# A routed expert layer behind attention on one core: weight casts, result turns and products in another order at each slot boundary

## The chip, the cores and the metric

The kernel runs on one core of a Trainium2 chip. The metric is the device time of one execution in microseconds (us). Before the change it was 924.96 us, the median of three runs from 918.28 to 929.62.

## What is computed

Attention with a causal mask and a decay bias on 8 x 8 heads of 576 x 64, then a two-level routed layer on the 4608 rows of 512 that come out of it: each row goes to the best of 4 groups and then to the best of 4 experts in it, and that expert (512 x 1024, relu, 1024 x 512) works on the row alone.

```python
scores = np.where(causal, -1e9, scale * q @ k.T + np.minimum(bias, 0.0))
x = (softmax(scores) @ v)            # rows of 512
g_idx = np.argmax(x @ w_group, axis=1)
for g in range(4):
    e_idx = np.argmax(xg @ w_expert[g], axis=1)
    for e in range(4):
        h = np.maximum(xg[mask_e] @ w1[g, e], 0.0)
        ye = h @ w2[g, e]
        out[tok_idx] = combined[:, None] * ye      # softmax weights of group and expert
```

## The kernel before

The first half of the span is attention and the routing that goes with it; the change leaves it alone. After it come 16 **slots**, one for each expert, the experts sorted by how many rows they got: slot k takes at most `CAPS[k]` rows, 368 in slot 1, falling to 256 in slots 14 and 15. The loop over slots 1 to 15 stands at L1463. All products are done to near fp32 accuracy from two halves: a tensor a is split into ah, its rounding to fp32r, and al = a - ah, and a product of a and b is ah x bh + al x bh + ah x bl, three matmuls.

For slot k the loop issues two halves:

- The **first half** (`h_items`, L1084): 8 items of 12 matmuls (L1107), item f giving 128 hidden columns in PSUM (ph). Behind each item ScalarE makes hh = relu(ph) rounded (L1102) and VectorE hl = relu(ph) - hh (L1103).
- The **second half** (`y_items`, L1147): 4 items of 24 matmuls (L1168), one for each 128 columns of y; ScalarE copies each out of PSUM into yT (L1165, L1179). Within the first item the products with hh come first (16), then the eight with hl. Where the cap is a multiple of 128 (slots 14 and 15) `y_rows` (L1120) takes another way, row blocks at once.

Beside these products three jobs run in pieces that the loop puts between the items:

- **W: the weights of the next slot.** Four tiles of 128 x 2048 (two of w1, two of w2) are loaded by the SP queue, each cut in four pieces, W[0] to W[15]. A piece is cast by ScalarE to wh (L997). Its low part wl is either subtracted by GpSimd (L1000), or ScalarE casts it once more into a PSUM tile pw (L1005) and VectorE subtracts that (L1007). For the last two tiles pieces 0 and 2 go to VectorE and pieces 1 and 3 to GpSimd. A tile's buffer is loaded anew three tiles later.
- **X: the rows of the next slot.** They have been gathered by a GpSimd DMA into xg (L953). In slots 2 to 14 sixteen 32 x 32 block transposes of VectorE turn them into xt (L1074; eight items of two), then two split items make xh (ScalarE, L1078) and xl = xt - xh (VectorE, L1079), half the columns each. Slots 1 and 15 use TensorE transposes (px, L1057) instead.
- **Z: the result of the slot before.** Sixteen VectorE transposes turn yT back into rows yr (L1221; eight items of two), then ScalarE scales them in two or three blocks (`leave`, L1224), and a GpSimd DMA scatters each (L958).

TensorE, VectorE and ScalarE run in the order in which the code is written (a manual schedule, L1462); a waiting instruction holds all that stand behind it on its engine. GpSimd's order and the SP queue's are the scheduler's. In the first half Z[i] and W[i] follow item i (L1468); in the second half four X items and two W pieces stand ahead of each of the first items, so X's two split items and W[12], W[13] stand ahead of item 2 and W[14], W[15] ahead of item 3 (L1478).

Of the kernel before, what the change touches and what calls it, by code (L numbers as in the profile page):

```python
# [8 lines left out]
F32 = mybir.dt.float32  # L9
# [4 lines left out]
ALU = mybir.AluOpType  # L14
# [6 lines left out]
P = 128  # L21
# [3 lines left out]
E = 16  # L25
# [67 lines left out]
def after(tc, *instructions):  # L93

    stack = ExitStack()
    for i in instructions:
        if i is not None:
            stack.enter_context(tc.issue_after(i.ins))
    return stack
# [824 lines left out]
def moe(tc, w1, w2, xs, st, out):  # L924
    nc = tc.nc
    V = nc.vector
    ident, mc = st.ident, st.cst
    with ExitStack() as ctx:
# [40 lines left out]
        class Expert:  # L969


            def __init__(self, u, e):
                self.u, self.e = u, e
                self.h, self.l, self.casts = [], [], []

            def load(self, hi=(None,) * 4, lo=(None,) * 4, eng=V):

                pieces = []

                with after(tc, *(loads[-1:] if 0 < self.u < E else ())):  # L980
                    e = nc.values_load(self.e, engines=[ENG.SP], min_val=0, max_val=E - 1)
                for i, w in enumerate((w1, w1, w2, w2)):

                    turn = 4 * self.u + i
                    q, n = (x1, 2) if turn % 3 < 2 else (x2, 1)
                    raw = q.tile([P, 4, 512], F32, name=f"raw{self.u}_{i}", tag="raw", bufs=n)
                    q, n = (wp, 4) if turn % 6 < 4 else (wq, 2)
                    h = q.tile([P, 4, 512], F32R, name=f"wh{self.u}_{i}", tag="wh", bufs=n)
                    l = q.tile([P, 4, 512], F32R, name=f"wl{self.u}_{i}", tag="wl", bufs=n)
                    self.h.append(h)  # L990
                    self.l.append(l)

                    def piece(j, i=i, w=w, raw=raw, h=h, l=l):
                        if j == 0:
                            loads.append(nc.sync.dma_start(raw, w[bass.ds(e, 1), i % 2].rearrange("o p a c -> p (o a) c")))
                        with after(tc, hi[i], lo[i]):
                            self.casts.append(nc.scalar.copy(h[:, j], raw[:, j]))  # L997

                            if (j in ((1, 2, 3) if i < 2 else (1, 3)) if eng is V else (i, j) not in lent):
                                self.low = lows[self.u, i, j] = nc.gpsimd.tensor_tensor(out=l[:, j], in0=raw[:, j],  # L1000
                                                                   in1=h[:, j].bitcast(F32), op=ALU.subtract)
                                return

                            ps = turn_in(f"pw{self.u}_{i}_{j}", F32R)
                            nc.scalar.copy(ps, raw[:, j])  # L1005
                            with after(tc, None if eng is V else st.valued if i == 2 else st.cut):
                                lows[self.u, i, j] = V.tensor_tensor(out=l[:, j], in0=raw[:, j], in1=ps.bitcast(F32),  # L1007
                                                                     op=ALU.subtract)

                    pieces += [lambda j=j, piece=piece: piece(j) for j in range(4)]  # L1010
                return pieces
# [10 lines left out]
        def acc(name):  # L1022

            turns[0] += 1
            return pm[turns[0] // 2 % 2].tile([P, 512], F32, name=name, tag="pm")
# [11 lines left out]
        class Slot:  # L1037
# [12 lines left out]
            def x_items(self):  # L1050
                u, cap = self.u, self.cap
                self.xh, self.xl = xhl(u, 0 if u == 0 else u + 1)

                def item(c):
                    ps = acc(f"px{u}_{c}") if u == 0 else turn_in(f"px{u}_{c}")
                    for t, r in enumerate(self.rows):
                        nc.tensor.transpose(ps[:, t * P:t * P + r], self.xg[:r, t, c * P:(c + 1) * P], ident[:r, :r])  # L1057
                    self.split = (nc.scalar.copy(self.xh[:, c, :cap], ps[:, :cap]),
                                  V.tensor_tensor(out=self.xl[:, c, :cap], in0=ps[:, :cap],
                                                  in1=self.xh[:, c, :cap].bitcast(F32), op=ALU.subtract))  # L1060

                if u < 2 or u == E - 1:
                    return [lambda c=c: item(c) for c in range(4)]

                xt = turned(u)
                nb = -(-cap // 32)

                def turn(j, i0):

                    n = len(range(j, nb, 4))  # L1070
                    for i in (i0, i0 + 1):
                        src = self.xg[32 * j:32 * j + 32].rearrange("p t (c i n) -> p t c i n", c=4, n=32)
                        dst = xt[32 * i:32 * i + 32].rearrange("p c (t j n) -> p t c j n", j=4, n=32)
                        V.transpose(dst[:, 0:n, :, j], src[:, 0:n, :, i])  # L1074

                def split(a):
                    xh, xl, x = (t[:, a:a + 2, :cap] for t in (self.xh, self.xl, xt))
                    nc.scalar.copy(xh, x)  # L1078
                    V.tensor_tensor(out=xl, in0=x, in1=xh.bitcast(F32), op=ALU.subtract)  # L1079

                return ([lambda j=j, i=i: turn(j, i) for j in range(4) for i in (0, 2)] +
                        [lambda a=a: split(a) for a in (0, 2)])

            def h_items(self):  # L1084
                u, cap = self.u, self.cap
                self.hh = hp.tile([P, 8, 384], F32R, name=f"hh{u}", tag="hh")
                self.hl = hp.tile([P, 8, 384], F32R, name=f"hl{u}", tag="hl")

                pss = {}

                def first(f):

                    pss[f] = acc(f"ph{u}_{f}")
                    for c in range(4):
                        for x in (self.xh, self.xl):
                            product(f, self.w.h, x, c)

                def last(f):
                    for c in range(4):
                        product(f, self.w.l, self.xh, c)  # L1100
                    ps, hh = pss.pop(f), self.hh[:, f, :cap]
                    self.rounded = self.rounds[f] = nc.scalar.activation(hh, ps[:, :cap], AF.Relu)  # L1102
                    self.rests[f] = V.scalar_tensor_tensor(out=self.hl[:, f, :cap], in0=ps[:, :cap], scalar=0.0,  # L1103
                                           in1=hh.bitcast(F32), op0=ALU.max, op1=ALU.subtract)

                def product(f, w, x, c):
                    self.product = nc.tensor.matmul(pss[f][:, :cap], w[f // 4][:, c, (f % 4) * P:(f % 4 + 1) * P], x[:, c, :cap],  # L1107
                                     start=(c == 0 and w is self.w.h and x is self.xh), stop=(c == 3 and w is self.w.l))

                def item(f):  # L1110
                    first(f)
                    last(f)

                if u == 0:

                    return [lambda f=f, part=part: part(f) for h in (0, 4) for part in (first, last)
                            for f in range(h, h + 4)]
                return [lambda f=f: item(f) for f in range(8)]
# [169 lines left out]
        def run(items):  # L1288
            for f in items:
                f()  # L1290
# [171 lines left out]
        with tc.manual_schedule(engines={ENG.PE, ENG.DVE, ENG.Activation}):  # L1462
            for k in range(1, E):  # L1463
                W = wts[k + 1].load() if k + 1 < E else []
                rest = beyond() if k + 1 == E else iter(())
                for i, f in enumerate(slots[k].h_items()):
                    f()
                    run(Z[i:i + 1] + W[i:i + 1])  # L1468
                    if k == 1 and i == 2:
                        by_slot(cws, cwl, 1, E)  # L1470
                    for _ in range(4):
                        next(rest, None)
                    if i == 4 and k + 2 < E:
                        slots[k + 2].gather()
                X = slots[k + 1].x_items() if k + 1 < E else []
                for i, f in enumerate(slots[k].y_items()):
                    n = 1 if k + 2 == E else 4
                    run((Z[8:] if i == 0 else []) + X[n * i:n * i + n] + W[8 + 2 * i:10 + 2 * i])  # L1478
                    f()
                Z = slots[k].z_items()  # L1480
            run(Z)
# [166 lines left out]
```

## Time and profile before

| | |
|---|---|
| Median of three runs | 924.96 us |
| The profiled execution's time | 921.04 us |
| Its span, first to last instruction | 919.3 us |
| TensorE matmul busy / weight load busy | 855.2 us (93%) / 780.2 us (85%) |
| VectorE busy | 736.9 us (80%) |
| ScalarE busy | 610.2 us (66%) |
| GpSimd busy | 605.7 us (66%) |
| Mean granted clock of TensorE | 0.986 of full speed |

How to read it: the shares are means over two very different halves. Slot 1 starts its products at 500.1 us; from slot 2 on (530.26 us) a slot is 24 to 30 us long, and what counts there is read slot by slot. Engines: PE is TensorE's matmul, PEld its weight load, DVE is VectorE, ACT is ScalarE, POOL is GpSimd. Successive matmuls start 0.12 to 0.17 us apart, while each is shown as 0.28 to 0.33 us long and its weight load as 0.19: the shown ends of matmuls reach into a wait behind them, those of weight loads hardly do.

### The profile page before, as it was taken

What the parts mean: (1) busy time and instruction counts of PE and PEld (TensorE: products, weight loads), DVE (VectorE), ACT (ScalarE), POOL (GpSimd) and SP (SyncE); (2) the same over time, 40 slices, a digit from 0 to 9 for tenths busy, and PEclk for the clock granted to TensorE, in tenths of its full rate; (3) what the DMA queues carried; (4) which work ended last, traced back from release to release, by engine and by line L of the source; (5) the groups of instructions that cost most, each with busy time, mean ns of one, the idle gap of its engine ahead of it and who ended that gap; (6) DMA issues with size and microseconds to landing.
All of it is one profiled execution on the core that took longest, in us unless ns stands there. A gap on an engine that the chain in (4) does not pass through costs nothing. (4 is left out here: it accounts for less than half of the span.)

```text
span 919.3 us, 17750 instructions
## 1 busy us (share of the span) xinstructions
PE 855.2 (93%) x5584; PEld 780.2 (85%) x5584; DVE 736.9 (80%) x1981; ACT 610.2 (66%) x1389; POOL 605.7 (66%) x748
## 2 busy tenths in 40 slices
PE   4899999999999999998798999999999999999995
PEld 2778788788888888886687999999999999999984
DVE  7666697787979798777578888899888899888871
ACT  5667777677777777775646566666767666767750
POOL 9666567666776758546665856766676776767650
PEclk9999999999999999999899999999999999999998
DMA  7899888888888888622544645545555545655510
GB/s 204 236 238 227 215 230 227 206 210 200 220 223 217 221 223 214 160 74 100 189 150 168 221 176 205 193 169 190 215 185 191 195 183 205 229 197 192 181 70 24
DMA packets 81877, 174.06 MB, mean 189 GB/s; under 512 B 9676, under 2 KB 45132, under 8 KB 73584
## 3 DMA queue, kind: packets, MB, share of 16 engines
q1 hardware_dynamic: 71664, 152.93, 57.8%
q0 software_dynamic: 7488, 18.89, 5.8%
q10 hardware_dynamic: 2624, 1.03, 0.5%
q8 instruction: 46, 0.75, 0.4%
q14 instruction: 55, 0.45, 0.2%
HBM read 108.97 MB, written 19.69 MB: 140 GB/s over the span
## 5 line engine op out<-in xcount | busy, mean ns | idle before, releaser
L1000 POOL TENSOR_TENSOR wl<-raw,wh 128x512 fp32r<-128x512 f32 x163 | 210.3, 1305 | 76.2 <-ACT wh L997 58.5
L227 DVE CUSTOM_DVE_ANT_0 mx<-pm,mask 128x192 bf16<-128x192 f32 (+4 forms) x320 | 127.3, 418 | 36.0 <-PE pm L219 33.3
L997 ACT CAST wh<-raw 128x512 fp32r<-128x512 f32 x256 | 155.3, 616 | 1.4 <-issue 1.4
L1107 PE MATMUL ph<-xl,wh 128*128 128x256 f32 (+13 forms) x512 | 145.3, 303 | 3.0 <-DVE xl L1079 3.0
L1107 PE MATMUL ph<-xh,wh 128*128 128x256 f32 (+13 forms) x512 | 144.8, 302 | 2.0 <-ACT xh L1078 1.7
L219 PE MATMUL pm<-WA 66*128 66x288 f32 (+4 forms) x384 | 124.8, 356 | 21.5 <-DVE mc L227 11.5
L275 PE MATMUL ps<-WA 68*128 68x320 f32 (+4 forms) x384 | 135.3, 356 | 4.8 <-DMA WA<-tl 4.6
L315 PE MATMUL po<-pt,VT 128*128 128x256 f32 (+3 forms) x512 | 120.9, 355 | 6.8 <-issue 4.2
L1168 PE MATMUL py<-hl,wh 128*128 128x256 f32 (+13 forms) x448 | 113.6, 302 | 1.7 <-DVE hl L1103 1.7
L1168 PE MATMUL py<-hh,wh 128*128 128x256 f32 (+13 forms) x448 | 112.9, 302 | 0.0
L277 PE MATMUL ps<-WB 128*128 128x320 f32 (+4 forms) x384 | 109.8, 299 | 0.0
L315 PE MATMUL po<-pu,VT 128*128 128x320 f32 (+1 forms) x384 | 107.5, 388 | 1.1 <-POOL pu L294 1.1
L1221 DVE STREAM_TRANSPOSE yr<-yT 32x384 f32<-32x384 f32 (+1 forms) x208 | 104.5, 502 | 4.2
L315 PEld LDWEIGHTS po<-pt,VT 128*128 128x128 f32 x512 | 88.4, 193 | 21.0 <-issue 5.0
L1074 DVE STREAM_TRANSPOSE xt<-xg 32x256 f32<-32x256 f32 (+1 forms) x208 | 102.5, 493 | 3.1
L1107 PEld LDWEIGHTS ph<-xl,wh 128*128 128x128 f32 x512 | 96.9, 189 | 5.9 <-DVE xl L1079 5.0
L1107 PEld LDWEIGHTS ph<-xh,wh 128*128 128x128 f32 x512 | 97.1, 190 | 3.8 <-ACT xh L1078 2.9
L219 PEld LDWEIGHTS pm<-WA 66*128 66x128 f32 (+1 forms) x384 | 69.1, 192 | 31.8 <-DVE mc L227 15.5
L294 POOL TENSOR_SCALAR_AFFINE_SELECT pt<-pt 128x128 f32<-128x128 f32 (+2 forms) x192 | 65.8, 354 | 43.7 <-ACT pt L285 40.5
L1102 ACT ACTIVATE hh<-ph 128x256 fp32r<-128x256 f32 (+13 forms) x128 | 53.6, 420 | 60.3 <-PE ph L1107 59.5
L161 POOL TENSOR_TENSOR WB<-r,hl 64x576 fp32r<-64x576 f32 x62 | 87.3, 1408 | 5.9 <-ACT hl L157 2.1
L1107 PE MATMUL ph<-xh,wl 128*128 128x256 f32 (+13 forms) x512 | 90.2, 299 | 0.0
(246 smaller groups left out, 2000.8 us busy)
## 6 DMA issues: line engine op xcount, KB each, us to landing
raw<-in_w_dram SPq DMA_DIRECT2D x64, 1024.0 KB
r<-in_qk_dram SPq DMA_DIRECT2D x32, 576.0 KB
WA<-hl SPq DMA_DIRECT2D x60, 288.0 KB
WB<-hl SPq DMA_DIRECT2D x60, 288.0 KB
VT<-in_v_dram SPq DMA_DIRECT2D x32, 384.0 KB
WB<-hl SPq DMA_DIRECT2D x64, 144.0 KB
xs<-xr SPq DMA_DIRECT2D x15, 512.0 KB
WA<-cumd SPq DMA_DIRECT2D x56, 4.5 KB
```

What stands on the lines that cost most here:

```text
L161: (nc.vector if p < 1 else nc.gpsimd).tensor_tensor(out=hl[:, 2] if part else WB[p % NBB][0:64, KA, h], in0=r[hr, part], in1=hl[hr, part]. ...
L219: nc.tensor.matmul(ps[:rows, :cw], WA[i][0:66, QA, h, QO + q0:QO + q0 + rows], WA[i][0:66, KA, h, QO + c0:QO + c0 + cw], start=True, stop= ...
L227: nc.vector.tensor_tensor_reduce(out=tmp[:rows, :cw], in0=ps[:rows, :cw], in1=mk[:rows], scale=1.0, scalar=-3.0e38 if c0 == 0 else mo, op0 ...
L275: nc.tensor.matmul(ps[:rows, o:o + w], WA[i][0:68, KA, h, QO + k0:QO + k0 + rows], WA[i][0:68, QA, h, QO + q0:QO + q0 + w], start=True, st ...
L277: nc.tensor.matmul(ps[:rows, o:o + w], WB[p % NBB][:, KA, h, k0:k0 + rows], WB[p % NBB][:, QA, h, q0:q0 + w], start=False, stop=True)
L315: nc.tensor.matmul(po[0][:, qa - base:qb - base], VT[p % NVT].rearrange("p t a d -> p (t a d)")[:, (3 * t + 1 + h) * 64:][:, 0:P], x[:, c: ...
L997: self.casts.append(nc.scalar.copy(h[:, j], raw[:, j]))
L1000: self.low = lows[self.u, i, j] = nc.gpsimd.tensor_tensor(out=l[:, j], in0=raw[:, j], in1=h[:, j].bitcast(F32), op=ALU.subtract)
L1074: V.transpose(dst[:, 0:n, :, j], src[:, 0:n, :, i])
L1107: self.product = nc.tensor.matmul(pss[f][:, :cap], w[f // 4][:, c, (f % 4) * P:(f % 4 + 1) * P], x[:, c, :cap], start=(c == 0 and w is sel ...
L1168: self.product = nc.tensor.matmul(pss[c][:, :cap], w[2 + f // 4][:, f % 4, c * P:(c + 1) * P], x[:, f, :cap], start=(f == 0 and w is self. ...
L1221: V.transpose(dst[:, 0:n, :, i], src[:, 0:n, :, j])
```

## The change

Five things move; no instruction is added or taken away, apart from the order.

- The last weight tile's four pieces W[12] to W[15] are all cast ahead of item 2 of the second half, and the split items of X move from item 2 to item 3, behind those casts. The low parts of these four pieces are held in a list (`held`) and issued right behind the split.
- GpSimd's first subtract on that tile is made to wait for VectorE's second split instruction (`hold`).
- The result turns of the slot before start two items earlier: Z[0] and Z[1] ahead of item 0, Z[2] to Z[7] behind items 0 to 5.
- In slots 2 to 14 the first item of the first half takes the products with xh first (with wh and wl), then the four with xl.
- In slot 14, X's transposes on TensorE stand ahead of the scaling of slot 13's rows.

```diff
@@ class Expert, load @@
+                            def pooled():
                                 self.low = lows[self.u, i, j] = nc.gpsimd.tensor_tensor(out=l[:, j], in0=raw[:, j],
                                                                    in1=h[:, j].bitcast(F32), op=ALU.subtract)
+                            if (j in ((1, 2, 3) if i < 2 else (1, 3)) if eng is V else (i, j) not in lent):
+                                if self.held is None:
+                                    pooled()
+                                else:
+                                    self.held.append(pooled)
                                 return
...
+                            def low():
+                                with after(tc, None if eng is V else st.valued if i == 2 else st.cut):
+                                    lows[self.u, i, j] = V.tensor_tensor(out=l[:, j], in0=raw[:, j], in1=ps.bitcast(F32),
+                                                                         op=ALU.subtract)
+                            if self.held is None:
+                                low()
+                            else:
+                                self.held.append(low)
@@ class Slot, h_items @@
                 def item(f):
+                    if f == 0 and 1 < u < E - 1:
+                        pss[f] = acc(f"ph{u}_{f}")
+                        for a in (0, 2):
+                            for w in (self.w.h, self.w.l):
+                                for c in (a, a + 1):
+                                    product(f, w, self.xh, c, False)
+                        for c in range(4):
+                            product(f, self.w.h, self.xl, c, c == 3)
+                        relu(f)
+                        return
                     first(f)
                     last(f)
@@ the loop over slots @@
                 for i, f in enumerate(slots[k].h_items()):
+                    if i == 0:
+                        run(Z[:2])
                     f()
-                    run(Z[i:i + 1] + W[i:i + 1])
+                    run(Z[2:8][i:i + 1] + W[i:i + 1])
...
                 for i, f in enumerate(slots[k].y_items()):
-                    n = 1 if k + 2 == E else 4
-                    run((Z[8:] if i == 0 else []) + X[n * i:n * i + n] + W[8 + 2 * i:10 + 2 * i])
+                    left = Z[8:] if i == 0 else []
+                    if k + 2 < E:
+                        if i == 2:
+                            wts[k + 1].held = []
+                        run(left + X[4 * i:4 * i + 4 if i < 2 else 0] +
+                            W[8 + 2 * i if i < 3 else 16:10 + 2 * i if i < 2 else 16])
+                        if i == 3:
+                            run(X[8:] + wts[k + 1].held)
+                            hold(tc, lows[k + 1, 3, 1], slots[k + 1].parted)
+                    else:
+                        run(X[i:i + 1] + left + W[8 + 2 * i:10 + 2 * i])
                     f()
```

(`relu(f)` is the two instructions that stood at the end of `last`, and `parted` is the second split's VectorE instruction.)

The order of ScalarE in the second half of slot 12, before. xh13 are the high rows of slot 13, wh13_3 and pw13_3 casts of its last weight tile, py12 the columns of y of slot 12, hh13 the first hidden values of slot 13:

```order
L1165 COPY yT_6564<-py12_1_11326 128x272
L1078 CAST xh13_11256<-xt13_11258 128x2x264 x2
L997 CAST wh13_3_11088<-raw13_3_11087 128x512
L1005 CAST pw13_3_0_11358<-raw13_3_11087 128x512
L997 CAST wh13_3_11088<-raw13_3_11087 128x512
L1165 COPY yT_6564<-py12_2_11363 128x272
L997 CAST wh13_3_11088<-raw13_3_11087 128x512
L1005 CAST pw13_3_2_11390<-raw13_3_11087 128x512
L997 CAST wh13_3_11088<-raw13_3_11087 128x512
L1165 COPY yT_6564<-py12_3_11395 128x272
L1102 ACTIVATE hh13_11444<-ph13_0_11446 128x264
```

And the same place now:

```order
L1194 COPY yT_6564<-py12_1_11326 128x272
L998 CAST wh13_3_11088<-raw13_3_11087 128x512
L1012 CAST pw13_3_0_11354<-raw13_3_11087 128x512
L998 CAST wh13_3_11088<-raw13_3_11087 128x512 x2
L1012 CAST pw13_3_2_11358<-raw13_3_11087 128x512
L998 CAST wh13_3_11088<-raw13_3_11087 128x512
L1194 COPY yT_6564<-py12_2_11361 128x272
L1092 CAST xh13_11256<-xt13_11258 128x2x264 x2
L1194 COPY yT_6564<-py12_3_11395 128x272
L1124 ACTIVATE hh13_11444<-ph13_0_11450 128x264
```

All six casts of the last tile have moved ahead of the copy of the third column and of xh; between xh and hh one copy is left.

The order of VectorE from the last hl of slot 12 to the second hl of slot 13, before. yr11 and yr12 are result turns, xt13 turns of the next rows, xl13 the split, wl13_3 the two subtracts on the last tile:

```order
L1103 SCALAR_TENSOR_TENSOR hl12_11091<-ph12_7_11237,hh12_11090 128x272
L1221 STREAM_TRANSPOSE yr11_11067<-yT_6564 32x8x32 x2
L1074 STREAM_TRANSPOSE xt13_11258<-xg1_6563 32x3x4x32 x4
L1074 STREAM_TRANSPOSE xt13_11258<-xg1_6563 32x2x4x32 x4
L1007 TENSOR_TENSOR wl13_2_11086<-raw13_2_11084,pw13_2_0_11281 128x512
L1074 STREAM_TRANSPOSE xt13_11258<-xg1_6563 32x2x4x32 x8
L1007 TENSOR_TENSOR wl13_2_11086<-raw13_2_11084,pw13_2_2_11321 128x512
L1079 TENSOR_TENSOR xl13_11257<-xt13_11258,xh13_11256 128x2x264 x2
L1007 TENSOR_TENSOR wl13_3_11089<-raw13_3_11087,pw13_3_0_11358 128x512
L1007 TENSOR_TENSOR wl13_3_11089<-raw13_3_11087,pw13_3_2_11390 128x512
L1103 SCALAR_TENSOR_TENSOR hl13_11445<-ph13_0_11446,hh13_11444 128x264
L1221 STREAM_TRANSPOSE yr12_11421<-yT_6564 32x12x32 x2
```

And now:

```order
L1125 SCALAR_TENSOR_TENSOR hl12_11091<-ph12_6_11222,hh12_11090 128x272
L1125 SCALAR_TENSOR_TENSOR hl12_11091<-ph12_7_11239,hh12_11090 128x272
L1088 STREAM_TRANSPOSE xt13_11258<-xg1_6563 32x3x4x32 x4
L1088 STREAM_TRANSPOSE xt13_11258<-xg1_6563 32x2x4x32 x4
L1016 TENSOR_TENSOR wl13_2_11086<-raw13_2_11084,pw13_2_0_11281 128x512
L1088 STREAM_TRANSPOSE xt13_11258<-xg1_6563 32x2x4x32 x8
L1016 TENSOR_TENSOR wl13_2_11086<-raw13_2_11084,pw13_2_2_11321 128x512
L1093 TENSOR_TENSOR xl13_11257<-xt13_11258,xh13_11256 128x2x264 x2
L1016 TENSOR_TENSOR wl13_3_11089<-raw13_3_11087,pw13_3_0_11354 128x512
L1016 TENSOR_TENSOR wl13_3_11089<-raw13_3_11087,pw13_3_2_11358 128x512
L1250 STREAM_TRANSPOSE yr12_11421<-yT_6564 32x12x32 x4
L1125 SCALAR_TENSOR_TENSOR hl13_11445<-ph13_0_11450,hh13_11444 128x264
```

The last two hl of a slot follow each other directly, and four result turns (two items) stand ahead of the first hl of the next.

## Rows read from the trace of the kernel before

**Rows 1.** Busy time by stretch: slots 5 to 13, then slot 14's halves.

```profile
core 0: us, PE busy (x) PEld busy (x) DVE busy (x) ACT busy (x) POOL busy (x), PEclk, DMA share, GB/s
617.86:645.60 27.74, 27.74 (x195) 27.74 (x193) 25.04 (x48) 18.25 (x39) 19.21 (x16) 1.00 0.52 192
645.60:673.05 27.45, 27.45 (x194) 27.05 (x193) 24.76 (x49) 18.41 (x40) 19.17 (x16) 1.00 0.55 197
673.05:700.87 27.82, 27.41 (x195) 26.90 (x193) 25.14 (x49) 18.81 (x40) 19.30 (x17) 1.00 0.55 194
700.87:728.14 27.27, 26.86 (x194) 26.49 (x193) 24.61 (x49) 18.79 (x40) 19.30 (x17) 1.00 0.57 199
728.14:755.26 27.12, 26.20 (x195) 25.41 (x193) 24.47 (x49) 18.65 (x40) 19.27 (x17) 1.00 0.55 197
755.26:781.81 26.55, 26.16 (x192) 25.69 (x192) 23.91 (x49) 18.60 (x40) 19.16 (x17) 1.00 0.57 201
781.81:808.31 26.50, 25.49 (x194) 24.74 (x193) 23.88 (x49) 18.55 (x40) 18.17 (x16) 1.00 0.56 199
808.31:834.69 26.38, 25.00 (x192) 24.26 (x193) 23.75 (x49) 18.41 (x40) 18.13 (x16) 1.00 0.56 201
834.69:860.42 25.73, 24.23 (x193) 23.52 (x193) 23.09 (x50) 18.25 (x40) 17.62 (x15) 1.00 0.57 203
860.42:872.90 12.48, 12.14 (x98) 11.88 (x99) 10.33 (x22) 11.00 (x25) 8.10 (x7) 1.00 0.57 191
872.90:886.25 13.35, 11.98 (x58) 9.54 (x56) 8.70 (x19) 9.63 (x21) 9.09 (x9) 1.00 0.23 95
```

**Rows 2.** What TensorE's weight loads waited for, 645.5 to 887: total, times, longest.

```profile
PEld ph L1107 <- DVE xl L1079: 5.0, 9, 0.6
PEld ph L1107 <- ACT xh L1078: 2.9, 6, 0.8
PEld py L1168 <- DVE hl L1103: 2.6, 4, 1.0
PEld px L1057 <- DVE xl L1059: 1.8, 1, 1.8
```

**Rows 3.** What VectorE waited for, 645 to 861 (slots 6 to 13).

```profile
DVE wl L1007 <- ACT pw L1005: 8.9, 8, 1.1
DVE hl L1103 <- ACT hh L1102: 3.8, 8, 0.5
DVE wl L1007 <- issue: 1.7, 8, 0.3
```

**Rows 4.** VectorE in order of time around the boundary of slots 12 and 13.

```profile
820.77 0.69 DVE L1007 TENSOR_TENSOR wl<-raw,pw 128x512 fp32r<-128x512 f32 x1
821.38 0.43 DVE L1103 SCALAR_TENSOR_TENSOR hl<-ph,hh 128x272 fp32r<-128x272 f32 x1
821.85 0.89 DVE L1221 STREAM_TRANSPOSE yr<-yT 32x256 f32<-32x256 f32 x2
822.77 0.44 DVE L1103 SCALAR_TENSOR_TENSOR hl<-ph,hh 128x272 fp32r<-128x272 f32 x1
...
825.55 4.11 DVE L1074 STREAM_TRANSPOSE xt<-xg 32x384 f32<-32x384 f32 x8
...
830.38 3.60 DVE L1074 STREAM_TRANSPOSE xt<-xg 32x256 f32<-32x256 f32 x8
...
834.67 1.33 DVE L1079 TENSOR_TENSOR xl<-xt,xh 128x528 fp32r<-128x528 f32 x2
```

**Rows 5.** ScalarE in order of time, the same boundary.

```profile
825.60 1.95 ACT L1224 ACTIVATE yr<-yr,cws 128x512 f32<-128x512 f32 x3 [3.28 <-issue]
827.46 0.60 ACT L997 CAST wh<-raw 128x512 fp32r<-128x512 f32 x1
...
829.01 0.37 ACT L1179 COPY yT<-py 128x272 f32<-128x272 f32 x1
...
834.01 1.17 ACT L1078 CAST xh<-xt 128x528 fp32r<-128x528 f32 x2 [2.78 <-DVE xt L1074]
```

**Rows 6.** GpSimd in order of time, the same boundary.

```profile
830.16 2.56 POOL L1000 TENSOR_TENSOR wl<-raw,wh 128x512 fp32r<-128x512 f32 x2
```

More of the change, by code (lines that the diff above doesn't have):

```diff
@@ L974, in __init__ @@
                 self.h, self.l, self.casts = [], [], []
+                self.held = None
             def load(self, hi=(None,) * 4, lo=(None,) * 4, eng=V):
@@ L997, in piece @@
                             self.casts.append(nc.scalar.copy(h[:, j], raw[:, j]))
-                            if (j in ((1, 2, 3) if i < 2 else (1, 3)) if eng is V else (i, j) not in lent):
+                            def pooled():
                                 self.low = lows[self.u, i, j] = nc.gpsimd.tensor_tensor(out=l[:, j], in0=raw[:, j],
                                                                    in1=h[:, j].bitcast(F32), op=ALU.subtract)
+                            if (j in ((1, 2, 3) if i < 2 else (1, 3)) if eng is V else (i, j) not in lent):
[3 more added lines that the diff above has]
+                                    self.held.append(pooled)
                                 return
@@ L1005, in piece @@
                             nc.scalar.copy(ps, raw[:, j])
-                            with after(tc, None if eng is V else st.valued if i == 2 else st.cut):
-                                lows[self.u, i, j] = V.tensor_tensor(out=l[:, j], in0=raw[:, j], in1=ps.bitcast(F32),
-                                                                     op=ALU.subtract)
+                            def low():
[6 more added lines that the diff above has]
+                                self.held.append(low)
                     pieces += [lambda j=j, piece=piece: piece(j) for j in range(4)]
@@ L1078, in split @@
                     nc.scalar.copy(xh, x)
-                    V.tensor_tensor(out=xl, in0=x, in1=xh.bitcast(F32), op=ALU.subtract)
+                    self.parted = V.tensor_tensor(out=xl, in0=x, in1=xh.bitcast(F32), op=ALU.subtract)
                 return ([lambda j=j, i=i: turn(j, i) for j in range(4) for i in (0, 2)] +
@@ L1100, in last, with product, relu @@
                         product(f, self.w.l, self.xh, c)
+                    relu(f)
+                def product(f, w, x, c, stop=None):
+                    self.product = nc.tensor.matmul(pss[f][:, :cap], w[f // 4][:, c, (f % 4) * P:(f % 4 + 1) * P], x[:, c, :cap],
+                                     start=(c == 0 and w is self.w.h and x is self.xh),
+                                     stop=(c == 3 and w is self.w.l) if stop is None else stop)
+                def relu(f):
                     ps, hh = pss.pop(f), self.hh[:, f, :cap]
@@ L1104, in last @@
                                            in1=hh.bitcast(F32), op0=ALU.max, op1=ALU.subtract)
-                def product(f, w, x, c):
-                    self.product = nc.tensor.matmul(pss[f][:, :cap], w[f // 4][:, c, (f % 4) * P:(f % 4 + 1) * P], x[:, c, :cap],
-                                     start=(c == 0 and w is self.w.h and x is self.xh), stop=(c == 3 and w is self.w.l))
                 def item(f):
+                    if f == 0 and 1 < u < E - 1:
[6 more added lines that the diff above has]
+                            product(f, self.w.h, self.xl, c, c == 3)
+                        relu(f)
+                        return
                     first(f)
```

## Prediction

> **What bounds the kernel now.** I read the busy time by slot first, then what TensorE and VectorE wait for in the same stretch, then one slot boundary on each engine. The reader should see in the first view that the slots fall in two kinds. A weight load overlaps the load before it while TensorE runs without a break, so the length of a slot less the PEld column is the time TensorE lost. In slot 5 (617.86 to 645.60) that is nothing: TensorE is the bound there [rows 1], and I take it for slots 2 to 4, which are larger. From slot 6 on it is 0.40, 0.92, 0.78, 1.71, 0.86, 1.76, 2.12 and 2.21 us for slots 6 to 13, together 10.76. In all eight, length less VectorE's busy time is 2.62 to 2.69 [rows 1]: from slot 6 on VectorE's cycle sets the length, and the smaller the slot, the more TensorE waits for it.
>
> The second view says where TensorE lost the time, to slot 14 inclusive: 5.0 for the low rows xl and 2.9 for the high rows xh at the first product of a slot, 2.6 for the last hl early in the second half, 1.8 in slot 14 for one transpose [rows 2], 12.3 in all. The third says what VectorE itself waited for in slots 6 to 13: ScalarE's cast of a last-tile piece into PSUM 8.9 + 1.7 ("issue" stands right before the other of the two pieces), and the first hh 3.8 [rows 3]. That is 14.4 us over 8 slots, 1.80 of the 2.64 in each. The other 0.84 lies in many gaps too short to be listed.
>
> Why this wait exists: in the old order ScalarE stands idle 2.78 us until VectorE's last turn of the next rows is done, then casts xh, and only then starts on the six casts of the last weight tile [rows 5], at the very boundary. So VectorE waits for the PSUM casts, and hh of the new slot comes after all six.
>
> **Part by part.**
>
> *Casts ahead of the split.* No cast is added or taken away; the six move into ScalarE's 2.78 us of idle. What does ScalarE need between VectorE's last result turn and the split? Three scalings 1.86 (825.60 to 827.46), then six casts of tile 2 and six of tile 3: three of them took 1.55 (827.46 to 829.01), so 6.20 for twelve; three copies at most 0.37 each, 1.11; start 0.05 [rows 5]. Sum 9.22. VectorE needs in the same time two hl at 0.47 (821.38 to 821.85) and the turns with one subtract, 825.55 to the last turn's end at 833.98, 8.43 [rows 4]: 9.37 in all. ScalarE is ready 0.15 us before it is wanted. That is a tie, and the cover is thin: if ScalarE is late by x, each slot is late by x. In slots that TensorE bounds the copy of the third y column holds the split instead; that one is done at about three quarters of the second half, three us before the boundary for 12.9 us halves, and two xh casts take 1.17 [rows 5].
>
> *Subtracts held back.* VectorE's two on the last tile stand behind the split with their PSUM casts long made: the waits of 8.9 and 1.7 go [rows 3]. GpSimd's two wait for the split. Its queue has two gathers ahead of them anyway, which wait for the same turns. Two subtracts take 2.56 [rows 6], so behind a split that ends at 1.3 they end about 4 us into the slot and are read a half slot later. I cost this at nothing; what hides it is the first half of the next slot, some 12 us.
>
> *Result turns moved up.* One group of four turns now stands ahead of the first hl, in the time in which VectorE waited 3.8 us for hh [rows 3], and the last two hl have no turns ahead of them. Walked for slot 13, from TensorE's first product: split done at 1.3 (834.67 + 1.33 [rows 4] against 834.69); two subtracts at 0.61, 2.5; four wide turns 2.3 (the eight turns of 4.11 less four narrow ones of 0.46), 4.8; first hl 5.3; five times a pair of turns 0.92 and an hl 0.47 with two subtracts among them, 13.4; last pair 14.4; two hl, 15.3 [rows 4]. TensorE wants the last hl after half of its 23.52 (11.76), 16 products of 0.1225 and 7 more: 14.6. So some 0.7 us of waiting stays in slot 13, which puts its end at 24.2, 0.3 beyond what VectorE's cycle asks (below). Slot 12 wants it at 15.0, and 24.26 + 0.3 stays inside VectorE's cycle. In larger slots it comes in time.
>
> *High rows first.* Twelve products as before, eight of them on xh. Eight of 0.1225 are 0.98 us in which the low rows need not be there; they come at 0.7 and 1.3. Of slot 14's 0.60 lost in its first half [rows 1] I leave 0.2 for the second xh and xl and count 0.4 as gained. In slots 6 to 13 this is part of the sum over whole slots.
>
> *Slot 14, transposes ahead of the scalings.* xh of the first transposed chunk stood behind three scalings that waited for the result turns, and the third transpose waited 1.8 for its xl [rows 2]; the window shows 13.35 - 11.98 = 1.37 of idle TensorE [rows 1]. With the chunk first and the result turns two groups earlier, it goes. I take 1.6, between the two.
>
> *Sum.* With VectorE's 1.80 of waiting gone, a slot lasts the longer of TensorE's work (PEld) and VectorE's busy time + 0.84: 27.05, 26.90, 26.49, 25.41, 25.69, 24.74 for slots 6 to 11 (TensorE's) and 24.59 and 23.93 for 12 and 13 (VectorE's) [rows 1]. Gains 0.40, 0.92, 0.78, 1.71, 0.86, 1.76, 1.79 and 1.80, the last less 0.3: 9.7. With 0.4 and 1.6 from slot 14: **11.7 us**. Slots 1 to 5, the attention ahead and slot 15 keep their time. The profiled execution took 921.04 (span 919.3, 1.7 around it): 909.3. It lies 3.9 under the median of the runs, 924.96; from there, 913.3.
>
> **The rivals.** *Part of VectorE's wait comes back.* The result turns that now lead need the last y column, which TensorE ends at the boundary and ScalarE copies after xh, 0.7 to 0.9 us in. In slots 12 and 13 VectorE gets there at 2.5, so nothing is lost; in 9 to 11 it may arrive before and stand up to 0.9, and ScalarE's tie may cost as much. Bounds: nothing, and 5 slots by 0.9 plus as much again in two of them, about 6. Gain then 6 us: 915 from the profiled execution, 919 from the median. Against it: slots 9 to 11 have VectorE slack of 0.02 to 0.94 that swallows part.
>
> *The split meets a subtract.* Before, the last GpSimd subtract of tile 2 ended at 832.72 and the split began at 834.67: 1.95 apart, so no row shows both at once [rows 4, 6]. If they met and one had to wait for the whole of the other, up to 1.28 us (half of 2.56) would go to VectorE in the five slots 9 to 13: 6.4 of the 11.7, leaving 5 us: 916, or 920 from the median. Against it: both follow the last result turn, and the new order puts two more hl between that turn and the split, so they move apart by 0.9. The Trainium skill, "SBUF — State Buffer", section "Who interferes with whom", states that a VectorE instruction with two SBUF inputs contends with a GpSimd instruction that reads SBUF; the split is such an instruction, and no run here shows them together. By that rule the hold is what keeps the last tile's subtracts off the split.
>
> *Nothing gained.* The order changes, but the bound is VectorE's work plus gaps I cannot see into (the 0.84 could grow in step). Then 921, or 925. Against it: 14.4 us are listed as waits with a releaser that the change removes.
>
> *Slower.* The place is ScalarE ahead of the split. If the twelve casts and three scalings end x us after VectorE's last turn, x is lost at each of nine boundaries, slots 6 to 14; it eats the 11.7 from x = 1.3 on. At x = 2 it is 18 - 11.7 = 6 us slower: 927, or 931. A late weight load or a late third y copy would do it. Against it: ScalarE was idle there by 2.78, and its casts of these tiles ran back to back.
>
> **How the numbers follow.** The forecast (gain 9 to 13) gets 0.62, a partial gain 0.18, the split meeting a subtract 0.04, nothing gained 0.11, slower 0.05. The predicted time is 913.3. The low end: all of 10.76 + 0.60 + 1.8 = 13.2 goes, from the fastest run of before, 918.28: 905. The high end: the partial gain of 6 from 928, between the median and the slowest run, 929.62: 922. Left out above it are slower runs of the last cases. Faster by over 2% asks for 18.5 us where TensorE loses 13 in all, so only the scatter of the measurement gives it 0.05; slower by over 2% is a part of the last rival, 0.03; within 2%, about what a measurement of this kernel can tell from no change, 0.92.
>
> **What would show it.** In the changed kernel the waits of VectorE for pw and hh should be gone and VectorE's idle per slot fall from 2.64 to about 0.9 in slots 12 and 13; TensorE's waits for xl, xh and the slot 14 transpose should vanish in slots 6 to 11 and 14; a wait of under 1 us for the last hl may stay in 12 and 13. Slot 13 should last about 24.2 instead of 25.73, slot 9 about 25.4 instead of 27.12, slots 2 to 5 as before. ScalarE idle before xh should be short. I am wrong if TensorE waits for xh in many slots with ScalarE busy right up to it, if VectorE stands before the first result turns, or if the split takes longer than 0.67 us a piece.

## The result and the profile after

The changed kernel takes 910.0 us (median of four runs, 908.1 to 911.9) against 921.6 for the kernel before (four runs, 918.2 to 929.6). The ratio is 0.985 with a 95% interval of 0.981 to 0.990, so between 9.5 and 18 us were gained. The prediction was 913.3 and a gain of 11.7; the medians lie 11.6 apart.

Busy time by stretch of the changed kernel: slots 6, 9, 10, 12 and 13, then slot 14's two halves, to be read against [rows 1]. Columns: stretch, its length, busy time of PE, PEld, DVE, ACT and POOL with the number of instructions, granted clock, DMA share, GB/s.

```profile
650.86:677.93 27.07, 27.07 (x195) 27.07 (x194) 24.98 (x49) 19.18 (x39) 19.98 (x18) 1.00 0.61 208
731.16:756.45 25.29, 25.29 (x195) 25.29 (x194) 23.95 (x49) 18.94 (x39) 18.65 (x16) 1.00 0.59 202
756.45:781.62 25.17, 25.17 (x195) 25.17 (x193) 23.58 (x49) 18.87 (x39) 19.44 (x18) 1.00 0.62 215
806.15:830.21 24.06, 24.06 (x194) 24.06 (x193) 23.29 (x49) 18.64 (x39) 17.46 (x16) 1.00 0.66 221
830.21:853.27 23.06, 23.06 (x194) 23.06 (x193) 21.96 (x47) 18.59 (x39) 17.85 (x15) 1.00 0.63 221
853.27:864.93 11.66, 11.66 (x99) 11.59 (x98) 11.24 (x24) 7.59 (x17) 6.80 (x7) 1.00 0.70 245
864.93:876.75 11.82, 11.82 (x58) 9.72 (x56) 7.96 (x16) 10.14 (x21) 9.81 (x9) 1.00 0.22 88
```

Length and PEld column are now the same in every slot from 6 to 13: TensorE loads weights without a break, and neither PE nor PEld has a listed wait between 535 and 877 us, where [rows 2] had 12.3. VectorE's idle, 2.62 to 2.69 in each slot before, is between 0.77 (slot 12) and 2.09 (slot 6), and now differs from slot to slot: it is no longer what sets the length. What VectorE waits for in slots 6 to 13 answers [rows 3]; the columns are total, times, longest:

```profile
DVE xl L1093 <- ACT xh L1092: 4.5, 7, 0.9
DVE hl L1125 <- ACT hh L1124: 0.7, 2, 0.4
DVE yr L1250 <- ACT yT L1194: 0.2, 1, 0.2
```

The waits for pw (8.9 + 1.7) are gone and those for hh fell from 3.8 to 0.7. In their place VectorE waits 4.5 for xh, a wait that was not there before.

Slots 2 to 5 last 115.3 us in both profiles, slots 6 to 13 214.82 before and 202.41 after, slot 14 25.83 and 23.48, and from slot 15's first product to the end 33.07 in both. That makes 14.8 us. The two profiled executions differ by only 9.5 (921.04 and 911.55) because the one of the changed kernel came to slot 2 5.3 us later, 535.54 against 530.26. Of these, 5.0 were there before slot 1's first product already (494.5 against 489.5 us; the 500.1 given ahead for the kernel before is wrong), in a part that the change leaves alone. In the profiles that follow slot 2 starts anywhere from 530.2 to 536.4, and the earliest, 530.2, is e9, which has the changed kernel's order up to slot 13: the delay is scatter, not the change. So I compare by the stretch from slot 6's first product to slot 14's ("slots 6 to 13" below); where nothing changed, such stretches repeat to 0.05 us.

### The profile page after: what moved, and what is told of

Its sections match the earlier page's. It is cut to its first block, busy times and chain, and to the rows that moved or that the text cites. A ratio compares the mean times of both kernels' runs of the same rounds, so it can differ in the third digit from the quotient of the medians.

```text
span 909.8 us, 17764 instructions
## 1 busy us (share of the span) xinstructions
PE 852.4 (94%) x5584; PEld 782.4 (86%) x5584; DVE 737.9 (81%) x1981; ACT 614.0 (67%) x1389; POOL 604.0 (66%) x748
## 5 line engine op out<-in xcount | busy, mean ns | idle before, releaser
L219 PE MATMUL pm<-WA 66*128 66x288 f32 (+4 forms) x384 | 125.2, 357 | 22.1 <-DVE mc L227 11.7
L1118 PE MATMUL ph<-xh,wh 128*128 128x256 f32 (+13 forms) x512 | 141.3, 302 | 0.3 <-DVE yr L1311 0.3
L1118 PE MATMUL ph<-xl,wh 128*128 128x256 f32 (+13 forms) x512 | 139.0, 302 | 0.0
L1118 PE MATMUL ph<-xh,wl 128*128 128x256 f32 (+13 forms) x512 | 92.1, 299 | 0.0
```

Of the source, the lines that this page charges most:

```text
L219: nc.tensor.matmul(ps[:rows, :cw], WA[i][0:66, QA, h, QO + q0:QO + q0 + rows], WA[i][0:66, KA, h, QO + c0:QO + c0 + cw], start=True, stop= ...
```

## The experiments

**The parts, one undone or one alone.**

e1 is the changed kernel with casts and split in the old order:

```diff
-                        if i == 2:
-                            wts[k + 1].held = []
-                        run(left + X[4 * i:4 * i + 4 if i < 2 else 0] + ...
-                        if i == 3: ...
+                        run(left + X[4 * i:4 * i + 4] + W[8 + 2 * i:10 + 2 * i])
```

> The changed kernel with one part undone: the six casts of the last weight tile stand behind the split again, two pieces ahead of item 2 and two ahead of item 3, and their subtracts follow at once, with no hold. Turns early, high rows first and slot 14's transposes first stay. Measure: from the first product of slot 6 to that of slot 14 (before 214.8 us, changed 202.4). My theory (VectorE's wait for the late PSUM casts sets the cycle of the slots): VectorE's wait for pw comes back at about 1.1 to 1.4 us a slot, and its first result turns now wait for the last y column behind the six casts, so its idle is again about 2.6 in slots 6 to 13: 211 to 215 us. Rival (TensorE's own waits for xl and hl were the cost, and products and turns cure them): the stretch stays within 2 us of the changed kernel's, 202 to 204.

e2 is the kernel before with the casts ahead, the subtracts held back and the hold, alone. As a diff against the changed kernel:

```diff
-                    if i == 0:
-                        run(Z[:2])
                     f()
-                    run(Z[2:8][i:i + 1] + W[i:i + 1])
+                    run(Z[i:i + 1] + W[i:i + 1])
...
-                    if f == 0 and 1 < u < E - 1:
+                    if False:
...
-                        run(X[i:i + 1] + left + W[8 + 2 * i:10 + 2 * i])
+                        run(left + X[i:i + 1] + W[8 + 2 * i:10 + 2 * i])
```

> The kernel before with one part alone: the last tile's six casts ahead of the split, its subtracts held back behind it, with the hold. Turns, product order and slot 14 as before. Measure: slots 6 to 13, 214.8 us before, 202.4 changed. My theory: most of the gain is here; VectorE's wait for pw is gone, that for the first hh stays (0.2 to 0.5 a slot where VectorE is ahead, and then it costs nothing): 202.4 to 206, and 9 to 12 us off the whole time, ratio about 0.987 to 0.990. Rival (the parts need each other: without the early turns the last hl is late, and without the high rows first TensorE waits for xl): 207 to 211 us, a ratio of 0.993 to 0.997.

e3 is the kernel before with the high rows first alone: of the change only the new `item` and what it calls.

> The kernel before with the high rows' products first in the first item, and slot-14 order, casts and turns as before. Measure: slots 6 to 13, 214.8 us before. My theory: TensorE's wait for xl goes (5.0 us in the weight loads' waits of before), but VectorE's cycle of busy time + 2.64 still sets the length, so the time is waited for elsewhere (xh, hl): 213.5 to 215. Rival (the wait for xl was a cost of its own): 209 to 211.

e4 is the changed kernel with the result turns in their old places (the first hunk of e2 alone).

> The changed kernel with the result turns in their old places (one group behind each of the eight items). Measure: slots 6 to 13, changed 202.4 us. My theory: VectorE waits some 0.2 to 0.6 us for the first hh again, but only where it is ahead of TensorE, so nothing or little is lost: 202.4 to 204; in slot 14 the scalings start later, 0 to 0.5 us. Rival (the early turns cure the late last hl, 2.6 us of TensorE's waits before): 205 or more, with TensorE waiting for hl in the second half.

The stretch of slots 6 to 13 in e1, e2, e3 and e4, columns as above:

```profile
646.83:856.31 209.48, 207.16 (x1539) 203.87 (x1537) 191.79 (x382) 147.51 (x309) 148.43 (x123) 1.00 0.58 202
```

```profile
646.93:854.77 207.84, 205.40 (x1538) 203.51 (x1536) 191.49 (x384) 150.52 (x312) 150.59 (x125) 1.00 0.58 205
```

```profile
647.66:862.52 214.86, 207.75 (x1539) 203.55 (x1537) 193.63 (x385) 147.88 (x313) 150.28 (x124) 1.00 0.56 199
```

```profile
646.31:852.04 205.73, 204.15 (x1539) 203.15 (x1537) 191.25 (x384) 150.48 (x312) 150.51 (x125) 1.00 0.59 207
```

e3 gives the cleanest answer: 214.86 against 214.82, nothing. Its weight loads waited, from slot 6 through slot 14's first products, for

```profile
PEld py L1197 <- DVE hl L1125: 6.8, 8, 1.2
PEld ph L1118 <- ACT xh L1092: 3.9, 8, 0.8
```

and VectorE's three rows of waits are those of [rows 3] to the digit (8.9, 3.8, 1.7). The wait for xl, 5.0 us before, is gone, and the wait for the last hl grew from 2.6 to 6.8. Removing a wait of the engine that waits for a slower one only moved it.

The casts alone (e2) gain 7.0 us in this stretch, and 0.989 in the whole time (0.981 to 0.997); the change without them (e1) gains 5.3; both together 12.4. So these two halves add up, and I was wrong about each: I gave casts 9 to 12 and all else little, and for e4 I expected at most 1.6 us where 3.3 were lost. Within the halves the parts do need each other, as the rival of e2 had it (207 to 211): e4 is e2 with the high rows first, as far as these slots go, and 2.1 us shorter, though the same order is worth nothing in the kernel before (e3) or with the turns early (e8, below). In e1 the old wait is back as I expected (8.9 for pw), but the first result turns wait only 1.2 us for the last y column where the first hl had waited 3.8 for hh; that was missing from my 211 to 215, and so was the lead (the time by which xh is done ahead of the slot's first product) that the larger slots build up: slots 6 to 8 of e1 keep the changed kernel's lengths to 0.01, and all 7.1 us are lost in slots 9 to 13.

**Why the early turns matter.** In e4 I had looked for the rival's sign, TensorE waiting for hl. There is none, though the time, 205.73, is the rival's; the weight loads in slots 6 to 14 wait for xh:

```profile
PEld ph L1118 <- ACT xh L1092: 2.4, 4, 1.4
PEld ph L1118 <- DVE xl L1093: 0.3, 1, 0.3
```

ScalarE and VectorE around e4's boundary of slots 12 and 13 (slot 13's first product at 827.35) show why. VectorE, in order of time, from slot 12's split over its last result turn to slot 13's split:

```profile
802.51 1.36 DVE L1093 TENSOR_TENSOR xl<-xt,xh 128x544 fp32r<-128x544 f32 x2 [0.54 <-ACT xh L1092]
...
816.77 0.90 DVE L1250 STREAM_TRANSPOSE yr<-yT 32x256 f32<-32x256 f32 x2
...
827.33 1.33 DVE L1093 TENSOR_TENSOR xl<-xt,xh 128x528 fp32r<-128x528 f32 x2 [0.51 <-ACT xh L1092]
```

ScalarE in the same stretch, from the scalings to xh:

```profile
817.75 1.95 ACT L1253 ACTIVATE yr<-yr,cws 128x512 f32<-128x512 f32 x3 [1.84 <-issue]
819.61 0.60 ACT L998 CAST wh<-raw 128x512 fp32r<-128x512 f32 x1
...
826.40 0.37 ACT L1194 COPY yT<-py 128x272 f32<-128x272 f32 x1
826.67 1.16 ACT L1092 CAST xh<-xt 128x528 fp32r<-128x528 f32 x2
```

The scalings stand at the head of ScalarE's queue and wait 1.84 us for the last result turn (it ends at 817.67, they start at 817.75; the row itself names no releaser, which is what "issue" means, so this is read from the times, and e10 tests it). Behind them the twelve casts run back to back up to xh. The split waits for xh, and the result turns of the next slot stand behind the split. This is a loop of two engines: 15.16 us on VectorE from split to last turn (802.51 to 817.67), 9.66 on ScalarE until the split can start (827.33), 24.82 together, and slot 12 of e4 lasts 24.83 where its products need 24.06. VectorE has no listed gap in its 15.16. The tie that I had worked out for ScalarE (9.22 and the first xh of 0.6) was its half of this loop.

e10 cuts the loop on ScalarE's side and leaves the turns late:

```diff
-                    left = Z[8:] if i == 0 else []
+                    left = Z[8:] if i == (1 if k + 2 < E else 0) else []
```

> The kernel e4 (changed, result turns in the old places; 205.7 us in slots 6 to 13) with one thing more: the three scalings of ScalarE stand behind the first y copy, two casts' pieces later, so that they no longer wait at the head of ScalarE's queue for the last result turn. Theory (a loop of two engines sets e4's late slots: VectorE from the split to the last result turn, 15.2 us in slot 12, then ScalarE's scalings, casts and xh, 9.6, together 24.8 where the slot is 24.83): the loop is cut, 202.4 to 203.5 us in slots 6 to 13, xh ready 0.5 us or more ahead of each first product. Rival (late turns cost through the last hl, whatever ScalarE does): 205 or more.

Its slots 6 to 13:

```profile
650.74:853.75 203.01, 202.82 (x1538) 202.50 (x1536) 191.32 (x384) 151.72 (x312) 151.07 (x125) 1.00 0.59 210
```

2.7 of the 3.3 us come back. Slots 6 to 12 have the changed kernel's lengths to 0.01; what is left is slot 13 with 23.67 instead of 23.06. Ahead of it xh follows VectorE's last turn directly, so there VectorE's own work is the limit. xh led the first product by 0.41 to 1.42 us in slots 6 to 12, where I had expected 0.5 or more, and by only 0.05 in slots 13 and 14.

e11 does the same to the changed kernel.

> The changed kernel with the scalings behind the first y copy. In the changed kernel the loop is 23.84 in slot 13, whose products take 23.06: xh's lead on the first product falls from 1.44 us (slot 13) to 0.63 (slot 14). Theory of the loop: here the lead into slot 14 stays at 0.9 or more, slots 6 to 13 keep 202.4 since nothing waited there, and slot 14 may gain up to 0.1. Rival (that lead is VectorE's own work, as the prediction had it): the lead falls to 0.6 all the same.

It fails the theory: 202.57 us in slots 6 to 13 (23.22 in slot 13 instead of 23.06), 23.68 in slot 14, and the lead into slot 14 fell to 0.43, not to 0.9. With the turns early the scalings hardly wait (0.27 us in slot 13 of the changed kernel, no listed wait in slots 6 to 12), and moved back they stand behind a y copy that itself waits 0.63 us for TensorE in slot 13, and push the later casts: the first xh ends 22.8 us into that slot instead of 22.4. The 0.16 that slot 13 lost stands before the products with its last hl. In the changed kernel the loop and VectorE's own cycle lie close together in slot 13: 23.84 from the split to the first xh's end, and 23.87 from split to split, of which VectorE waits 0.32 for xh. Neither can be called the next bound by these runs alone.

**How much cover ScalarE has.** e7 casts the last tile's four wh pieces twice, the same value each time:

```diff
                             self.casts.append(nc.scalar.copy(h[:, j], raw[:, j]))
+                            if self.held is not None:
+                                self.casts.append(nc.scalar.copy(h[:, j], raw[:, j]))
```

> The changed kernel with four casts of ScalarE more ahead of each split (the last tile's four wh pieces are cast twice), 4 x 0.52 = 2.08 us of ScalarE a slot. It measures the cover that ScalarE has there. In the changed kernel xh ends 2.2 us (slot 6) to 1.4 us (slot 13) before the slot's first product and 0.6 before slot 14's. Theory A (ScalarE's chain behind the last result turn is a tie with VectorE's, as forecast, but TensorE is ahead of neither: its cover is that 0.6 to 2.2): slots 6 to 13 lose 0.5 to 3 us, 203 to 205.5, slot 14 begins late by most of 1.4. Theory B (no cover, each us on ScalarE is a us in each slot): 8 x 2.08 = 16.6 more, 219. Theory C (ScalarE still has idle time there): 202.4.

Slot 13 of e7, columns as above, and what its weight loads waited for at the nine boundaries into slots 6 to 14:

```profile
847.04:874.21 27.17, 25.02 (x192) 24.70 (x192) 23.51 (x49) 21.00 (x44) 16.04 (x14) 0.94 0.58 200
```

```profile
PEld ph L1120 <- ACT xh L1094: 11.9, 9, 2.4
PEld ph L1120 <- DVE xl L1095: 5.6, 13, 0.7
```

Slots 6 to 13 last 224.14, 21.7 more, beyond even theory B's 16.6 and far from my 0.5 to 3. The loop explains it: in slot 13, split to last turn is 14.97 and last turn to the first xh's end 12.17, together 27.14 against the slot's 27.17; in the changed kernel 14.23 and 9.60, 23.84 before rounding. The casts bring 2.57 of that, and the split, which here meets a GpSimd subtract, 0.7. In the other slots the second part is 12.2 to 12.6, except 13.4 in slot 10, where TensorE's clock fell (last section), so a share of that slot's loss is the clock's. The lead that I counted as cover, 0.6 to 2.2 us, is spent once and is not there again in each slot, since the next slot's turns start later by as much.

**The hold.** e5 holds both GpSimd subtracts on the last tile, e6 none:

```diff
                             hold(tc, lows[k + 1, 3, 1], slots[k + 1].parted)
+                            hold(tc, lows[k + 1, 3, 3], slots[k + 1].parted)
```

> The changed kernel with the hold on both of GpSimd's subtracts on the last weight tile, not on one. In the changed kernel four split instructions last 1.95, 2.54, 2.13 and 1.15 us instead of 0.68 to 0.87 (at the boundaries into slots 3, 4... the larger ones, and 14), each while a GpSimd subtract runs. My theory (the scheduler put the subtract that isn't held ahead of the held one, and a split with two inputs in SBUF stands while GpSimd reads there): with both held every split lasts 0.68 to 0.87; TensorE had cover, so slots 2 to 13 keep their length (2 to 5: 115.3, 6 to 13: 202.4) and slot 14 loses at most 0.1 of its 23.48. Rival (the long splits come from something else, as the gathers): they stay over 1.1 us.

> The changed kernel without the hold. My theory: where no gather stands ahead of them on GpSimd, both subtracts can meet the split, at the boundaries that show a long split already, and at no others, since elsewhere two gathers that wait for VectorE's turns come first; splits of 1.1 to 3.3 us there; TensorE's cover (0.2 to 2 us from the end of the split to its first use) takes most of it: slots 2 to 5 115.3 to 116.5, slots 6 to 13 202.4 to 203.5, slot 14 23.5 to 24.5. Rival (the hold is what keeps every split clear): long splits at most boundaries and 205 us or more in slots 6 to 13.

The changed kernel at the boundary into slot 3, VectorE's split and then GpSimd's two subtracts on the last tile:

```profile
563.42 3.30 DVE L1093 TENSOR_TENSOR xl<-xt,xh 128x664 fp32r<-128x664 f32 x2 [1.41 <-ACT xh L1092]
```

```profile
563.94 1.30 POOL L1001 TENSOR_TENSOR wl<-raw,wh 128x512 fp32r<-128x512 f32 x1
566.81 1.29 POOL L1001 TENSOR_TENSOR wl<-raw,wh 128x512 fp32r<-128x512 f32 x1 [1.56 <-DVE xl L1093]
```

One subtract runs inside the split and only the second waits for it. The two parts of the split take 2.54 and 0.84 us there. The same place in e5:

```profile
564.27 1.61 DVE L1093 TENSOR_TENSOR xl<-xt,xh 128x664 fp32r<-128x664 f32 x2 [1.40 <-ACT xh L1092]
```

```profile
566.12 2.53 POOL L1001 TENSOR_TENSOR wl<-raw,wh 128x512 fp32r<-128x512 f32 x2 [1.34 <-DVE xl L1093]
```

With both held the split takes 1.61 and both subtracts come after it. So the hold covers half of what it looks like: the scheduler put the subtract without a hold first. In e6, which has none, the split into slot 5 takes 4.11 us:

```profile
616.52 4.11 DVE L1093 TENSOR_TENSOR xl<-xt,xh 128x628 fp32r<-128x628 f32 x2 [1.25 <-ACT xh L1092]
```

What does it cost? Slots 6 to 13 last 202.41, 202.40 and 202.42 us in the changed kernel, e5 and e6: nothing, since there the second of the two gathers that stand ahead of the subtracts and wait for VectorE's turns ends after the split in every slot; in e6 it ended before or inside the split into slots 2 and 5. Slots 2 to 5 are 115.3, 115.3 and 115.9; slot 14 23.48, 23.36 and 23.45. This is as expected but for slot 14, where e5 gained 0.12 and did not lose, and e6 came out 0.05 under its range. The hold is worth 0.6 us, in slots 2 to 5.

**The two small parts.** e8 is the changed kernel with the first item's products by turns (`if False:` as in e2).

> The changed kernel with the first item's products in the old order, high and low rows by turns. My theory: in slots 6 to 13 of the changed kernel the split ends 0.1 to 0.7 us before the first product, so the order costs nothing there: 202.4 to 202.7; into slot 14, where the split ends 1.2 us late, 0.4 to 0.8 us; slots 2 to 5, where a GpSimd subtract makes the split late into slots 3 and 5, 0 to 0.6. Rival (the order is worth as much as TensorE's wait for xl was, 5.0 us): 205 or more in slots 6 to 13.

e9 has slot 14's transposes behind the scalings again (the last hunk of e2).

> The changed kernel with slot 14's transposes behind the scalings again, as before. My prediction put 1.6 us on this part (slot 14 lasts 23.48 changed, so 25.1). New theory, after the first runs: the third transpose waited in the kernel before because the last result turns, and so the scalings, were late; with the turns early, xh of the first chunk comes at about 3.3 us into the second half instead of 1.4, its low rows before the third transpose at 6.2: 23.4 to 23.7, no wait of px.

e8 lasts 202.41 in slots 6 to 13, 0.4 more in slots 2 to 5 and 24.13 in slot 14, 0.65 more:

```profile
PEld ph L1118 <- DVE xl L1093: 0.9, 3, 0.5
```

That row covers slots 2 to 14. The high rows first pay only where the split is late: into slot 14, and where the split meets a subtract. e9 lasts 202.40 and 23.51 in slot 14: this part is worth 0.03 us.

## Why the prediction was right, point by point

**The bound.** Right. From slot 6 on VectorE's cycle, not TensorE's work, set the length, and the waits that the change removes were its cause (e1, e2); e3 shows what helping TensorE alone is worth, 0.0.

**Casts ahead of the split.** The step held, in its price too: 9.22 us were forecast from the last result turn to xh's start, e4's rows have 9.0 (817.67 to 826.67). But "a tie" was read as harmless. In e2 and e4, where the turns are late, ScalarE's half of the loop is what TensorE waits for; the place of the slower rival was real, and the early turns kept it from deciding. In the changed kernel VectorE does wait 4.5 us for xh, but TensorE, which has no listed wait, lost nothing by it.

**Result turns moved up.** Wrong reason. I gave them the first wait for hh and the last hl. Their worth, 3.3 us on top of the casts and the high rows (e4), is mostly that the scalings behind them start sooner; with the scalings out of the way 0.6 of it is left (e10).

**High rows first.** Right for the change as a whole: nothing of its own in slots 6 to 13 (e8), and 0.65 in slot 14 where I had 0.4. That it is worth 2.1 us when the turns are late (e2 against e4) I had not seen.

**Slot 14's transposes.** Wrong term. The 1.6 us were gained, slot 14 lost all of its waits, but not by this edit (0.03, e9). What cured the third transpose's wait of 1.8 was first of all the casts: in e2, with the old order and the turns late, the weight loads' row for it is down to

```profile
PEld px L1071 <- DVE xl L1073: 0.3, 1, 0.3
```

and the early turns take the rest (e9 has no such row, in the old order).

**The sum.** It was 9.7 for slots 6 to 13 and 2.0 for slot 14; measured were 12.4 and 2.35. Two terms were too small. For slots 12 and 13 I charged VectorE's cycle in full, 24.59 and 24.2; they took 24.06 and 23.06. The cycle itself was well sized for slot 13 (from split to split 23.87, 0.32 of it the wait for xh; forecast 23.93), but VectorE entered that slot 1.4 us ahead, xh done at 828.77 for a first product at 830.21, and spent 0.8 of it. A cycle that is longer than TensorE's in two slots only is paid from the lead that the slots before leave; that is 1.7 of the 2.7 us. The rest lies in slots 8 to 11, slot 10 above all (25.17 for a PEld of 25.69): weight loads are shown 0.19 long and start 0.13 apart, so each gap shows 0.06 shorter in that column than it is, and TensorE's work was put too high. In slot 10 of the kernel before the loads moreover start 0.133 us apart on average outside the gaps, in the changed kernel 0.131: 0.36 us, whose cause these runs don't show. So the 13.2 that the prediction took for all that could go was no ceiling: the profiles gave 14.8. That the medians lie 11.6 apart, next to the forecast 11.7, is luck: the part ahead of slot 2, which the change does not touch, scatters by 6 us and hid the difference.

**The split meets a subtract.** It happened, at other boundaries (2, 3, 5 and 14) and with another subtract, the last tile's, which I took to be held. It was one of the signs of being wrong that I had named, and it cost TensorE at most the 0.12 that e5 regains. The rule of the Trainium skill that the prediction names ("SBUF — State Buffer", section "Who interferes with whom": a VectorE instruction with two SBUF inputs contends with a GpSimd instruction that reads SBUF) agrees with these rows: the split has two inputs in SBUF, and a part of it took 2.54 us instead of 0.84 while GpSimd read.

**Hold at nothing.** Right; the subtracts end within 4 us of the split and nobody waited for them.

No run beat the changed kernel beyond what a run can tell: TensorE has no listed wait left in slots 2 to 14, and e5 gains 0.12 us.

## What to carry over

When a fast engine waits at a stage's boundary, find which engine is behind and what that one waits for; a reorder that helps only the fast engine moves its wait (e3). Before calling a step covered, follow it round: work that waits at the head of an in-order queue for the end of the stage before, and whose successors feed the next stage's start, closes a loop whose length is the stage's (e4, e7), and a lead over it is spent once, not once a stage. A hold on one of two like instructions leaves a scheduler free to run the other first.

## What the runs showed of the hardware that I had not expected

A VectorE subtract with both inputs in SBUF stretches from 0.84 to 2.54 us when a GpSimd subtract of 1.30 us starts during it, more than the whole of the other instruction, while GpSimd's own time stays at 1.30. At all four boundaries (2, 3, 5 and 14) the long part ends 0.55 to 0.74 us after the subtract, 0.12 to 0.14 less than it takes alone, although into slot 2 the subtract had started 0.1 us before it and into slot 3 0.52 after it. So starting first did not save the split; why is not shown. GpSimd's gathers beside it changed nothing: in the kernel before, splits beside gathers took the 0.67 us a piece of [rows 4].

In e7 TensorE's weight loads waited about two us at each boundary (11.9 and 5.6 over nine), and at three of the nine, into slots 10, 13 and 14, its granted clock fell: 0.94 over slot 13 (the row above), one stretch of 3.4 us at 1.2 GHz right behind the boundary and the rest at 2.4. Into these three the longest single wait was 1.8, 2.2 and 2.4 us; into slot 12, where it was 1.95, the clock stayed. In slots 6 to 14 of the kernel before, whose waits were at most 1.0 us long at the boundaries and 1.8 once [rows 2], it stayed at 1.00.
